# Linear attention and a maxout layer on one core: one transfer for each stored tile, a new order of the last fifth, and a last chunk that is stored by column halves

## The chip, the cores and the metric

The kernel runs on one core of one Trainium2 chip. The time is that of one execution on the device in microseconds (us); several runs are taken, and their median is compared. Besides these runs one execution is recorded by the hardware profiler, and all views shown here come from such records. The engines are TensorE (PE, with its weight loads as PEld), VectorE (DVE), ScalarE (ACT), GpSimd (POOL) and SyncE (SP), which here only issues transfers. The transfers run on 16 DMA engines.

## The reference

Eight batches of eight heads, 576 positions, head dimension 64. First a linear attention with a feature map of 2 x 128 features, then a feed-forward layer with the maximum of three products:

```
def phi(x):
    proj = einsum('bhsd,df->bhsf', x, w_phi)
    proj = proj - max(abs(proj), axis=-1, keepdims=True)
    return concatenate([exp(proj), exp(-proj)], axis=-1)
q_p, k_p = phi(q), phi(k)
kv  = einsum('bhsf,bhsd->bhfd', k_p, v);   z = sum(k_p, axis=2)
num = einsum('bhsf,bhfd->bhsd', q_p, kv)
den = einsum('bhsf,bhf->bhs', q_p, z)[..., None] + 1e-06
x   = (num / den), transposed and reshaped to (4608, 512)
h   = maximum(maximum(x @ w1, x @ w2), x @ w3)     # (4608, 768)
out = h @ w_out                                    # (4608, 512) float32
```

## The kernel before

**Attention** runs over 16 units of four heads (`attention`); two units make a batch. A unit's q, k and v come in as float32 tiles (`raw`), q and k are cast to bf16 (`qk_bf`) and transposed by a DMA (`qkT<-qk_bf`, line 524; in the first units by PE). The row maxima of the q projection, transposed on PE into `mT` (18 rows), are written by a small DMA into a row of `qkT` (`qkT<-mT`, line 582), from where a matmul subtracts them (`psm`, line 626). The divided results (`x_sb`) are transposed by another DMA into `xT` (`xT<-x_sb`, line 703).

**Which token lies where.** A partition holds nine consecutive positions of a batch, so tile c of a batch has the positions 9 i + c for i from 0 to 63. The first eight of the nine tiles of each batch make a chunk of 512 tokens; the ninth tiles of all eight batches are copied by POOL into `x_last` (line 965) and make a ninth chunk. An output tile of 128 rows of chunk b is thus two runs, c = 2 tt and c = 2 tt + 1, of 64 rows each. In the output tensor the rows of a run lie nine rows apart, and the second run starts one row after the first.

**The feed-forward layer** runs over these nine chunks (`chunk`). Differences of the weights are prepared, so that the maximum becomes one relu and one maximum: per chunk twelve groups of matmuls (`ups`, line 848), each taken out of PSUM into `hT` by ACT or DVE. Chunks 0 to 4 then compute each output tile directly (`ops`, lines 879 and 884), copy it to a tile `osb` and store it (line 899). Chunks 5 to 8 (`FAST`) use a scheme with seven products instead of eight (`fast`): POOL forms sums of quarters (line 760), PE the products p1 to p7 (`fps`, line 795), and DVE joins them by additions (`add`, line 802) into two `raw` tiles: `low` holds output rows 0 to 255 of the chunk, `high` rows 256 to 511, each as [128, 2, 512]. In column halves these are the four quarters c11, c12 (low) and c21, c22 (high). They are stored at line 827.

**Stores.** Each stored tile of 128 rows leaves in `n_out` transfers: two of 64 rows in chunks 0 to 7 (one for each run of positions), one of 128 rows in the ninth chunk. SP issues them; in the ninth chunk ACT issues two of the four. SP's queue also carries the loads, the two kinds of transposes and most of the `mT` transfers, in the order in which it issues them.

**The order of all work** is written out by hand: `PLAN` (lines 98 to 253) is a list of steps, each a node's number, a letter for its engine (T PE, D DVE, A ACT, G POOL, S SP) and its buffer slots, with a planned start. `plan` emits each engine's instructions in that order; the planned times set nothing else but the small filler matmuls of the first microseconds (`fill`). PSUM has eight banks, `raw` eight slots; a step that writes a slot waits until the slot's last readers, stores among them, are done.

Of the kernel before, what the change touches and what calls it, by code (L numbers as in the profile page):

```python
# [12 lines left out]
ALU = mybir.AluOpType  # L13
AXX = mybir.AxisListType.X

B, H, S, D = 8, 8, 576, 64
DF = 128
DM = H * D
# [99 lines left out]
199A@37.90 151D1@37.97 194A0@38.05 154T5@38.05 189A@38.30 233T2@38.36 195S@38.45 82D@38.59 180A@38.64 364G@38.78 156T7@38.81  # L118
# [18 lines left out]
318A@67.59 392T4@67.73 1133T@67.79 305D@67.94 393A0@68.08 313A@68.33 321D@68.55 1300G@68.82 1138D3@69.15 414T037@69.19
1134A2@69.34 394A@69.95 559G2@70.02 322T42@70.23 307T16@70.35 882S4@70.50 325D@70.60 415A@70.65 1152T0@70.68 311D@70.94
688S6@70.96 323A@71.05 560G@71.14 687S7@71.42 310D@71.54 1140T3@71.55 308A@71.69 298S1@71.88 326D@72.15 416A@72.18 1127S@72.34
1142T4@72.42 324A@72.64 1141D0@72.67 309A@72.98 306D@73.28 327T7@73.29 1146T1@73.35 328A1@73.60 1153D@73.88 329S@74.00  # L140
330A1@74.03 304A@74.28 432T003200@74.31 333G1@74.43 1147D@74.50 447T67@74.55 558S2@74.70 494G@74.71 433A@74.80 1154T0@74.87
450D@75.11 751S5@75.16 449A@75.29 1143D@75.72 405T10@75.74 448A@75.80 1158T6@75.96 428S3@75.98 406A@76.29 1155D@76.35 407A@76.79
1150T5@76.83 451D@76.97 434A@77.28 1159D@77.58 1148T4@77.70 1151A@77.95 436D@78.20 1144T0@78.57 435D@78.80 411T7@79.44
332G@79.50 1162T1@79.56 413A@79.81 1145A@80.15 1160T6@80.43 1149A@80.65 1163D@80.68 412A@81.15 399T5@81.30 408T0@81.52
1161D@81.55 331G@81.59 402T2@81.74 401A@81.77 1156T3@81.96 561S1@82.21 400A@82.28 403A@82.76 1172T1@82.83 1157D@83.08 404A@83.27
690G1@83.68 409A@83.75 437T47@83.80 452T56@84.04 340T31@84.25 438A@84.29 455D@84.41 1173T@84.47 440D@84.75 454A@84.78 410A@85.12
441D@85.35 686S1@85.57 453A@85.60 349T125@85.86 342A@85.94 1174D1@86.02 1135S@86.03 439A@86.43 456D@86.64 442T40@86.90
341A@86.92 350D@87.15 417T70@87.23 1175S@87.23 443A@87.40 445D@87.53 346T1@87.55 1164T6@87.67 348A@87.92 418D0@88.14 347A@88.28
1139S@88.43 343T2@88.54 351D@88.76 421T3@88.76 754G2@88.93 345A@89.01 334T4@89.08 337T1@89.30 422D1@89.33 356T71@89.52
496S2@89.77 338A@89.77 423T5@89.84 357D0@90.09 1165T@90.16 339A@90.28 446D@90.71 335A@90.76 689G@90.86 344A@91.25 424D1@91.32  # L150
419T3@91.46 336A@91.73 354T1@91.78 420D0@92.03 358T7@92.10 444A@92.22 1168T2@92.42 355D1@92.65 1166A2@92.71 425S@92.97
359D0@93.27 352T4@93.29 460A0@93.32 463A0@93.59 572T110511@93.71 461G@93.72 353D1@93.89 567T63@93.94 562T17@94.18 568A@94.43
1169T@94.51 575D@94.51 360S@94.66 573A@94.92 570D@95.12 569A@95.41 566D@95.72 462G@95.81 574A@95.90 577T40@95.90 881S7@96.16
1176T6@96.23 571D@96.33 1170A1@96.39 621S5@96.62 580D@96.94 579A@97.00 1177T@97.10 563A@97.49 565D@97.55 564A@98.00 576D@98.15
457T3@98.40 582T24@98.55 479T017@98.67 458A0@98.71 581D@98.76 583A@98.96 459S@99.11 584A@99.32 585D@99.37 578A@99.66
502T005300@99.71 586D@99.81 622S1@99.81 1182T2@100.04 481D@100.15 493S3@100.27 590A1@100.30 480D@100.53 1178A3@100.55
591G1@100.70 506D@100.91 512T47@101.01 507T10@101.24 1179S@101.31 515D@101.52 1190T6@101.57 509A@101.73 510D@102.12 504A@102.22
1186T4@102.44 1167S@102.51 514A@102.71 1183D1@102.73 593G@102.79 592G@103.07 508A@103.20 1188T1@103.31 505D@103.34 503A@103.69
511D@103.95 513A@104.18 1200T2@104.18 1189D@104.55 1187A@104.67 467T30@105.05 1465G@105.16 1191A@105.17 1201D@105.30
817S2@105.31 609T150@105.37 1306G@105.56 468A@105.67 469A@106.17 497T12@106.41 517T46@106.64 610A@106.66 625G0@106.76  # L160
1184T3@106.85 500D@106.89 611A@107.06 519A@107.46 516D@107.50 476T0@107.72 587T5@107.84 624G@107.88 1198T1@107.90 477A@108.09
520D@108.11 1185D@108.45 478A@108.45 470T7@108.77 588A1@108.79 464T4@108.99 501D@109.06 589S@109.19 473T0@109.21 471A@109.24
1196T5@109.43 465A@109.73 626S0@109.89 472A@110.21 1202T3@110.30 1197D@110.55 474A@110.70 486T70@111.17 475A@111.20 1203D@111.42
1194T5@111.49 466A@111.69 487D0@112.04 498A@112.17 600T01@112.36 1180T3@112.58 1195D@112.66 499A@112.68 816S1@113.09 602A@113.17
1199D@113.28 522T4@113.45 597T7@113.51 601A@113.68 603T2@113.73 521D@113.90 482T5@113.95 604A@114.20 1181D@114.24 1208T1@114.27
605A@114.71 483D1@114.85 488T0@115.14 525A0@115.19 598A@115.44 594T3@115.46 523D0@115.47 526G0@115.59 1192T5@115.68 489D0@115.71
524S@115.82 518A@115.93 599A@116.27 623S5@116.52 484T2@116.55 596A@116.75 1193D@116.80 1204T4@116.87 1171S@116.98 595A@117.26
485D1@117.42 528G@117.69 637T110611@117.84 527G@117.97 632T75@118.07 1131S@118.18 640D@118.32 532T20@118.40 634A@118.56
541T3@118.62 1209T@118.74 543A@119.05 636D@119.20 542A@119.41 534A@119.75 641D@119.81 606T0@120.04 884G0@120.06 538T3@120.16
533A@120.26 1205T@120.38 691S1@120.41 635D@120.41 540A@120.74 1210D3@121.02 885G@121.18 633A@121.23 529T2@121.68 539A@121.72  # L170
1206D2@121.93 544T071@122.00 530A@122.20 1301G@122.30 531A@122.71 627T53@123.04 545D@123.29 546A@123.29 535T4@123.37
1466G@123.50 1212T2@123.59 490S@123.61 630D@123.67 537A@123.84 1303G@123.90 631D@124.27 536A@124.34 549T71@124.46 547T1@124.78
550D0@125.03 629A@125.03 553T5@125.10 752S3@125.11 551T4@125.42 638A@125.52 548D1@125.65 1213T@125.74 628A@126.01 552D0@126.27
608A@126.50 607A@126.86 554D1@126.89 642T73@127.13 639A@127.20 702T001400@127.37 645D@127.62 555S@127.66 647T05@127.66
704A@127.85 1216T6@127.87 651D@128.22 1214A1@128.34 705D@128.56 614T70@128.74 644A@128.95 1217T@129.06 886S2@129.16 650D@129.17
703A@129.44 615D0@129.51 648A@129.93 706D@130.13 649A@130.29 652T2@130.36 697T10@130.51 1218A0@130.63 653D1@130.74 692T75@130.78
700D@131.00 707T42@131.09 694A@131.27 1230T6@131.42 646D@131.61 699A@131.76 710D@132.21 1222T1@132.29 654S@132.36 655A1@132.36
656G1@132.76 1231D0@132.82 946S7@133.06 1224T4@133.16 1223D@133.43 883S4@133.52 1234T6@134.03 695D@134.04 1225A@134.28
# [123 lines left out]
def kernel(  # L302
# [439 lines left out]
    def fast(b, ready, hT, evac, out_rows, ff, n_out):  # L742
# [268 lines left out]
```

## Time and profile before

| | |
|---|---|
| median of 3 runs | 283.24 us (282.25 to 283.63) |
| profiled execution, its own time | 282.29 us |
| its span, first to last instruction | 280.5 us |
| PE busy | 270.9 us (97%) |
| DVE, ACT, POOL busy | 224.0, 191.3, 168.5 us |
| granted clock of TensorE, mean | 0.996 |
| DMA packets, bytes, mean rate | 68050, 51.46 MB, 183 GB/s |
| stores on SP: `osb` tiles, `raw` tiles of 64 rows | 40 and 24 transfers of 128 KB |
| stores of the ninth chunk | 4 transfers of 256 KB, two on SP and two on ACT |

The span lies inside the time of a run; what is left, 1.8 us, lies around it. A busy PE is one with matmuls in flight, so its share alone does not say that it works at its best. The page cuts the span into 40 slices, one digit for each; 9 means 90% or more. A DMA share is the mean over the 16 DMA engines and can pass 1, since packets overlap. In a row of waits the column after the colon is the total, then how often and the longest.

### The profile page before, as it was taken

The numbers are of one execution on the slowest core, as the hardware profiler recorded it, in microseconds if no ns is written. First come the engines' busy times: TensorE is split into PE (matmuls) and PEld (weight loads), VectorE is DVE, ScalarE is ACT, GpSimd is POOL, SyncE is SP. The second block draws the span as 40 slices with busy tenths as digits, with TensorE's granted clock in tenths as the row PEclk, the third lists the DMA queues.
The fourth block names the chain that finished last, engine by engine and source line by source line (L and its number), as shares of the span: only waits on it lengthen the run. The fifth ranks groups of instructions, "written<-read, shape, count | busy, mean of one in ns | idle before, by whom it ended". The sixth has DMA issues, their size and how long they took to land.

```text
span 280.5 us, 8829 instructions
## 1 busy us (share of the span) xinstructions
PE 270.9 (97%) x3663; PEld 164.1 (58%) x3663; DVE 224.0 (80%) x466; ACT 191.3 (68%) x439; POOL 168.5 (60%) x147
## 2 busy tenths in 40 slices
PE   8899999999999999999999999999999999999991
PEld 3566774465546555564556456565485589444881
DVE  4899899988869997889898878897589565756292
ACT  3799997798879988898684699887654860112000
POOL 8075787839444764570768079267875892927910
PEclk9999999999999999999999999999999999999998
DMA  7999999997999997799899729984232108245037
GB/s 212 234 211 320 266 224 197 384 277 139 287 382 245 197 313 251 193 204 227 240 263 156 194 49 261 202 201 89 51 78 49 40 18 118 55 95 116 0 89 212
DMA packets 68050, 51.46 MB, mean 183 GB/s; under 512 B 48746, under 2 KB 52650, under 8 KB 68010
## 3 DMA queue, kind: packets, MB, share of 16 engines
q1 hardware_dynamic: 63561, 45.41, 66.2%
q0 software_dynamic: 4000, 4.92, 10.3%
q8 instruction: 28, 0.46, 0.6%
q10 hardware_dynamic: 449, 0.57, 0.6%
q14 instruction: 12, 0.10, 0.1%
HBM read 34.64 MB, written 9.44 MB: 157 GB/s over the span
## 4 chain that ended last, share of the span: by engine, by line
PE 78%; DMA 9%; DVE 6%; ACT 3%; issue 1%; POOL 1%; DVEq 0%; POOLq 0%; ACTq 0%
PE ups L848 33%; PE fps L795 8%; PE ops L884 7%; PE psn L673 5%; PE kvps L655 5%; PE ops L879 5%; PE psq L547 5%; PE psm L626 5%; DMA qk_bf<-in_k_dram 3%; DMA qkT<-qk_bf 3%; DMA qkT<-mT 3%; ACT Eq L639 2%; DVE raw L802 2%; PE pm L950 2%; PE tps L509 1%; DVE mqp L566 1%
## 5 line engine op out<-in xcount | busy, mean ns | idle before, releaser
L601 POOL TENSOR_TENSOR vab<-raw,em 128x1152 bf16<-128x1152 f32 (+1 forms) x36 | 68.1, 1906 | 69.4 <-ACT em L597 55.1
L560 ACT ACTIVATE Ek<-psk 128x512 bf16<-128x512 f32 (+1 forms) x160 | 82.2, 568 | 13.8 <-PE psk L547 10.0
L848 PE MATMUL ups<-xT,w_bf 128*128 128x512 bf16 x384 | 90.8, 379 | 0.0
L639 ACT ACTIVATE Eq<-psm 128x512 bf16<-128x512 f32 (+1 forms) x160 | 79.4, 571 | 10.4 <-PE psm L626 9.6
L848 PEld LDWEIGHTS <-w_bf 128*128 128x128 bf16 x432 | 41.0, 98 | 46.4
L566 DVE TENSOR_REDUCE mqp<-psq 128x4 bf16<-128x512 f32 (+1 forms) x80 | 49.2, 634 | 8.4 <-PE psk L547 5.7
L566 DVE TENSOR_REDUCE mk<-psk 128x4 f32<-128x512 f32 (+1 forms) x80 | 48.9, 630 | 1.1 <-ACT Ek L560 0.5
L855 DVE TENSOR_TENSOR hT<-hT,ups 128x512 bf16<-128x512 bf16 x54 | 36.2, 684 | 16.8 <-PE ups L848 13.9
L857 ACT ACTIVATE hT<-ups 128x512 bf16<-128x512 f32 x28 | 16.6, 606 | 30.1 <-PE ups L848 30.0
L680 DVE TENSOR_TENSOR x_sb<-psn,rden 128x320 bf16<-128x320 f32 x64 | 31.5, 492 | 2.2
L492 POOL CAST qk_bf<-raw 128x1152 bf16<-128x1152 f32 x24 | 27.2, 1148 | 5.8 <-DMA qkT<-qk_bf 3.5
L673 PEld LDWEIGHTS <-Eq 128*128 128x128 bf16 x640 | 24.7, 97 | 7.5 <-ACT Eq L639 0.7
L884 PE MATMUL ops<-wout_bf,hT 128*128 128x512 bf16 x120 | 29.1, 379 | 0.0
L673 PE MATMUL psn<-kv_sb,Eq 128*128 128x65 bf16 x640 | 26.8, 194 | 0.5 <-ACT Eq L639 0.5
L547 PE MATMUL psq<-w,qkT 64*128 64x128 bf16 x288 | 24.5, 217 | 1.0 <-DMA qkT<-qk_bf 0.6
L547 PE MATMUL psk<-w,qkT 64*128 64x128 bf16 x288 | 24.1, 217 | 0.2
L547 PEld LDWEIGHTS <-qkT 64*128 64x128 bf16 x576 | 16.6, 94 | 12.7 <-issue 8.9
L626 PE MATMUL psm<-qkT,wphi_m 128*128 128x512 bf16 (+1 forms) x70 | 22.3, 359 | 0.5 <-DMA qkT<-mT 0.3
L879 PE MATMUL ops<-xT 128*128 128x512 bf16 x80 | 20.6, 380 | 0.0
L859 DVE TENSOR_SCALAR hT<-ups 128x512 bf16<-128x512 f32 x26 | 17.5, 684 | 3.8 <-PE ups L848 3.6
L655 PE MATMUL kvps<-vab,Ek 64*128 64x65 bf16 x1152 | 20.2, 190 | 0.0
L655 PEld LDWEIGHTS <-Ek 64*128 64x128 bf16 x1152 | 18.8, 94 | 2.3 <-DVE mk L566 0.4
(97 smaller groups left out, 333.8 us busy)
## 6 DMA issues: line engine op xcount, KB each, us to landing
raw<-in_v_dram SPq DMA_DIRECT2D x16, 576.0 KB
raw<-in_q_dram SPq DMA_DIRECT2D x12, 576.0 KB
raw<-in_k_dram SPq DMA_DIRECT2D x12, 576.0 KB
out_dram<-osb SPq DMA_DIRECT2D x40, 128.0 KB
out_dram<-raw SPq DMA_DIRECT2D x24, 128.0 KB
w_bf<-in_moe_w_dram POOLq DMA_DIRECT2D x3, 768.0 KB, 9.4
qk_bf<-in_q_dram POOLq DMA_DIRECT2D x3, 288.0 KB, 8.2
qk_bf<-in_k_dram POOLq DMA_DIRECT2D x3, 288.0 KB, 9.3
```

The costliest lines, as they stand in the source:

```text
L547: nc.tensor.matmul(ps()[:, i, :], lhsT=cols[r, :], rhs=w2[r, c, :], start=True, stop=True)
L560: nc.scalar.activation(Ek[s]()[:, tiles_of(t0, n), :], of(1), EXP, scale=1.0 - 2.0 * s)
L566: nc.vector.tensor_reduce((mq, mk)[c]()[:, tiles_of(t0, n)], of(c), AXX, ALU.max, apply_absolute_value=True)
L601: (nc.vector if n_.eng == "DVE" else nc.gpsimd).tensor_tensor(vab()[:, g, t0:t1, 0:D], vb()[:, t0:t1, :], em()[:, g, t0:t1].unsqueeze(2).t ...
L626: nc.tensor.matmul(psm()[:, 0:w], lhsT=wphi_m, rhs=rhs, start=True, stop=True)
L639: nc.scalar.activation(Eqb()[s][:, cols], psm()[:, 0:w], EXP, scale=1.0 - 2.0 * s)
L655: nc.tensor.matmul(kvps[ab]()[:, t // NT, g, :], lhsT=Ek[g]()[r, t, :], rhs=vab()[r, g, t, :], start=(t + g == 0), stop=(t == UT - 1 and g ...
L673: nc.tensor.matmul(psn()[:, c, :], lhsT=Eqb()[g][:, t0:t0 + P], rhs=kv()[:, pr, ab, g, :], start=(g == 0), stop=(g == 1))
L848: nc.tensor.matmul(ups(), lhsT=w_bf[i + 1][:, ct, j * P:(j + 1) * P], rhs=tokens_of(ct), start=(ct == 0), stop=(ct == CT - 1))
L855: nc.vector.tensor_tensor(hT()[:, j, :], hT()[:, j, :], ups(), ALU.max)
L879: nc.tensor.matmul(ops_()[:, 0:width], lhsT=tile_of(ct, tt), rhs=line_w[:, ct, cols], start=(ct == 0), stop=False)
L884: nc.tensor.matmul(ops_()[:, 0:width], lhsT=hT()[:, j, tt * P:(tt + 1) * P], rhs=wout_bf[:, j, cols], start=False, stop=(j == JT - 1))
```

## The change

Three parts.

1. Stores of chunks 0 to 7: the two transfers of 64 rows become one of 128 rows, which writes the two runs as [2, 64, 512].
2. The ninth chunk: product p4, which completes c21, is split into its two row tiles, each in a PSUM bank of its own with an addition of its own. Its results leave in five transfers instead of four: c11, c12 and c22 (256 rows of 256 columns each), then the two halves of c21 (128 rows of 256 columns each), dealt to SP and ACT.
3. `PLAN` is new for the last fifth, and slightly so before: three of the `x_last` copies on POOL come earlier (at places planned for 65, 90 and 120 us instead of 105, 124 and 211). From about 238 us on, chunk 7's `ups` groups come before those of chunk 8, ACT takes all twelve relus of the two chunks, and products, additions and stores of both stand in another order.

The code, without the table:

```diff
-        def product(a, w, s):
-            ps = bank("fps", [P, 2, HF])
+        def product(a, w, s, halves=(0, 1)):
+            ps = bank("fps", [P, len(halves), HF])
             def mm(ps=ps, a=a, w=w):
-                for p in range(2):
+                for k, p in enumerate(halves):
                     for c in range(5):
-                        nc.tensor.matmul(ps()[:, p, :], lhsT=a(c, p), rhs=w(c), start=(p + c == 0), stop=(p + c == 5))
+                        nc.tensor.matmul(ps()[:, k, :], lhsT=a(c, p), rhs=w(c), start=(k + c == 0),
+                                         stop=(k == len(halves) - 1 and c == 4))
...
-        p4 = product(a_of(1, 1), t_of(3), None)
-        n_21 = add(lambda: p4, [n_7, n_22], c21, c21, [high])
+        n_21 = []
+        for halves in ((0,), (1,)) if b == B else ((0, 1),):
+            p4 = product(a_of(1, 1), t_of(3), None, halves)
+
+            def c21_of(halves=halves):
+                return high()[:, halves[0]:halves[-1] + 1, 0:HF]
+            n_21.append(add(lambda p4=p4: p4, [n_7, n_22], c21_of, c21_of, [high], 0.07 + 0.28 * len(halves)))
...
-        for tt in range(SM // P):
-            o2, need = (low, [n_11, n_12]) if tt < 2 else (high, [n_21, n_22])
+        parts = [(low, 0, 2, 0, HF, n_11), (low, 0, 2, HF, DM, n_12), (high, 0, 2, HF, DM, n_22),
+                 (high, 0, 1, 0, HF, n_21[0]), (high, 1, 2, 0, HF, n_21[-1])]
+        for o2, p0, p1_, c0, c1, need in parts if b == B else []:
+            def last(n_, o2=o2, p0=p0, p1_=p1_, c0=c0, c1=c1):
+                whole = out.rearrange("(r c) n -> c r n", c=NT)[NT - 1]
+                t0 = HT * (o2 is high)
+                queue_of[n_.eng].dma_start(whole[t0 + p0 * P:t0 + p1_ * P, c0:c1].rearrange("(t p) n -> p t n", p=P),
+                                           o2()[:, p0:p1_, c0:c1])
...
+        for tt in range(0 if b == B else SM // P):
+            o2, need = (low, [n_11, n_12]) if tt < 2 else (high, n_21 + [n_22])
...
-              lambda tt, rows=rows: [(rows[2 * tt + i], slice(i * ST, (i + 1) * ST)) for i in range(2)], 2)
+              lambda tt, rows=rows: [(rows[2 * tt:2 * tt + 2], slice(0, P))], 1)
```

Of the table, one line of the end before and one now:

```diff
-1458D@268.23 1507T6@268.73 1453D@268.85 1464S@269.00 1456D@269.49 1509T5@269.82 1508D3@270.11 1463S@270.20 1512D@270.75
+1511T4@271.10 1510D3@271.66 1522S@271.81 1514T2@272.19 1512D@272.44 1513D@273.15 1516T3@273.28 1518T1@273.82 1515D@273.84
```

SP's queue between the attention of the middle batches and the end, as a difference (a row is the line, what is written and from what, the shape that is written, and how often it stands there in a row):

```order
 L524 DMA_TRANSPOSE qkT<-qk_bf 128x18x128
 L486 DMA raw<-in_v_dram 128x2x576 x2
-L899 DMA out_dram<-osb 64x512 x4
+L915 DMA out_dram<-osb 2x64x512 x2
 L703 DMA_TRANSPOSE xT<-x_sb 128x10x128 x2
 L582 DMA qkT<-mT 1x18x128
```

Nothing has moved against its neighbours; each pair of stores is one, and its shape has a new outermost count of 2. At the queue's end, where only stores are left:

```order
 L703 DMA_TRANSPOSE xT<-x_sb 128x10x128
-L827 DMA out_dram<-raw 64x512 x22
-L827 DMA out_dram<-raw 128x512 x2
+L843 DMA out_dram<-raw 2x64x512 x11
+L834 DMA out_dram<-raw 128x2x256 x2
+L834 DMA out_dram<-raw 128x256
```

Eleven stores of the new shape stand ahead of the three parts of the ninth chunk that SP issues. DVE's last additions, of the ninth chunk, before (osb_5773 is the chunk's intermediate, raw_5731 its `low`, raw_5789 its `high`, each fps a product):

```order
L802 TENSOR_TENSOR osb_5773<-fps_5747,raw_5731 128x512
L802 TENSOR_TENSOR raw_5731<-fps_5735,osb_5773 128x2x256
L802 TENSOR_TENSOR raw_5789<-fps_5762,osb_5773 128x2x256
L802 TENSOR_TENSOR raw_5789<-fps_5735,raw_5789 128x2x256
L802 TENSOR_TENSOR raw_5789<-fps_5778,raw_5789 128x2x256
L802 TENSOR_TENSOR raw_5731<-fps_5793,raw_5731 128x2x256
L802 TENSOR_TENSOR raw_5731<-fps_5808,raw_5731 128x2x256
```

and now (osb_5747, raw_5721 and raw_5761 are the same three tiles):

```order
L803 TENSOR_TENSOR osb_5747<-fps_5725,raw_5721 128x512
L803 TENSOR_TENSOR raw_5721<-fps_5710,raw_5721 128x2x256
L803 TENSOR_TENSOR raw_5761<-fps_5736,osb_5747 128x2x256
L803 TENSOR_TENSOR raw_5721<-fps_5750,osb_5747 128x2x256
L803 TENSOR_TENSOR raw_5761<-fps_5750,raw_5761 128x2x256
L803 TENSOR_TENSOR raw_5721<-fps_5764,raw_5721 128x2x256
L803 TENSOR_TENSOR raw_5761<-fps_5777,raw_5761 128x256
L803 TENSOR_TENSOR raw_5761<-fps_5783,raw_5761 128x256
```

`low`'s left half is now finished second instead of last but one, and the last two additions, into `high`, are halves of what was one.

More of the change, by code (lines that the diff above doesn't have):

```diff
@@ L137 @@
[L137 to L154, printed above, removed]
@@ L248 @@
[L248 to L252 removed]
+381D@61.25 283A@61.50 390D@61.86 282A@61.86 218T0@61.98 1126A1@62.23 278T5@62.30 291T61@62.52 219D1@62.55 289T4@62.84
@@ new lines @@
+441D@85.54 453A@85.79 686S1@85.86 349T125@86.05 342A@86.13 1174D1@86.20 1135S@86.32 439A@86.61 456D@86.82 1175S@86.97
+442T40@87.09 341A@87.10 350D@87.34 417T70@87.42 1139S@87.52 443A@87.59 445D@87.72 346T1@87.74 1164T6@87.86 348A@88.11
+418D0@88.33 347A@88.47 343T2@88.73 351D@88.95 421T3@88.95 345A@89.20 754G2@89.22 334T4@89.27 337T1@89.49 422D1@89.52
+356T71@89.71 338A@89.96 496S2@89.96 423T5@90.03 357D0@90.28 1466G@90.34 1165T@90.35 339A@90.46 446D@90.90 335A@90.95 344A@91.43
+424D1@91.50 419T3@91.65 689G@91.84 336A@91.92 354T1@91.97 420D0@92.22 358T7@92.29 444A@92.40 1168T2@92.61 355D1@92.84
@@ new lines @@
+955D@189.03 1469G@189.04 849S@189.27 969A@189.49 956D@189.64 972T74@189.70 869T153@189.82 1294A3@189.98 975D@190.24
+962T20@190.86 957T61@191.09 870A@191.11 871D@191.11 1338G7@191.20 857T70@191.42 965D@191.49 958A@191.58 863T3@191.64
+1326T5@191.86 960D@192.09 865A@192.11 1336G@192.40 858A@192.60 976D@192.70 1334T2@192.73 961D@193.04 864A@193.08 859A@193.57
+1015G@193.60 1314T6@193.60 966D@193.65 980A0@194.40 860T3@194.47 1322T7@194.69 1315D0@194.72 981G0@194.80 1016S0@194.87
+862A@194.94 1327D@195.35 861A@195.45 1318T6@195.56 1323A@195.93 1320T3@196.43 1319A@196.68 1309G@196.90 963A@197.18
@@ new lines @@
+1312T7@197.30 1321D@197.55 1337G@197.57 866T6@198.17 1330T5@198.29 1313D@198.42 867A@198.54 1311G@198.77 868A@198.90
+1324T3@199.16 1331D@199.41 982G@199.44 854T7@200.03 1335D@200.03 1332T5@200.25 855A@200.50 1325D@200.65 856A@201.01
+1316T6@201.12 1333D@201.37 974A@201.49 1339G@201.53 959A@201.83 1328T7@201.99 1317A@202.32 964A@202.82 876T20@202.86
+1329D@203.11 872T3@203.18 983A@203.31 973A@203.46 878T1@203.50 877D0@203.73 874T6@203.82 1340G3@203.88 1344T5@204.14
+873D1@204.35 875D0@204.97 1357T7@205.23 1345A6@205.48 879D1@205.59 1341G@205.63 880S@206.36 1027T112011@206.42 1022T43@206.65
@@ new lines @@
+1017T61@206.89 1028A@206.90 1030D@206.90 1350T5@207.22 1342G4@207.36 1029A@207.41 1025D@207.51 1299S@207.86 1018A@207.90
+1020D@208.12 977T2@208.31 1346T4@208.37 1295S@208.41 1019A@208.41 1031D@208.72 1024A@208.90 1468G@209.09 1348T6@209.46
+1026D@209.54 1387G1@209.79 1347D0@210.15 1373T0@210.55 1351D@210.79 1343G@210.99 1349D2@211.41 1363T4@211.42 978D1@212.03
+1358D@212.23 1369T6@212.29 979A@212.38 1389G@212.72 1364D1@212.85 1365T2@213.16 1370A@213.41 1352D@213.46 1374D@214.08
+999T074@214.12 1366A@214.28 1021D@214.69 1023A@214.78 1032T56@215.16 1037T20@215.40 1001A@215.41 993T31@215.61 1035D@215.65
@@ new lines @@
+1034A@215.81 1371T1@215.83 1041D@216.25 994A@216.30 1036D@216.59 987T4@216.70 995A@216.81 1381T5@216.92 1040D@217.20
+1372A@217.29 1375T3@217.79 1039A@217.79 1382D@218.04 1045A1@218.13 989A@218.38 1046G1@218.53 1042T1@218.66 1367T2@218.72
+1000A@218.87 1043D0@218.97 1376D@219.17 988A@219.27 1044S@219.32 984T5@219.59 1377T7@219.81 1368A@219.84 1291S@220.02
+985A@220.34 1047G@220.62 990T4@220.68 986A@220.84 1355T1@220.90 1378D@220.93 992A@221.33 996T3@221.99 1385T2@222.11 1356D@222.24
+998A@222.36 1048A@222.70 1471G@222.72 997A@222.85 1379T5@222.98 11G@223.12 991A@223.19 1386D@223.23 1388G@223.27 1033A@223.67
@@ new lines @@
+1072D1@231.62 1074D0@232.24 1067T7@232.46 1397T1@232.78 1068D1@233.03 1075S@233.80 1408T5@233.87 1395T3@234.96 1401T2@236.05
+1396D0@236.30 1398D2@236.93 1404T7@237.14 1472G@237.23 1409D@237.57 1438G7@237.63 1400D4@238.19 1414T3@238.23 1403D@238.83
+1439G@238.85 1416T1@239.10 1415A0@239.35 1407D@239.47 1426T5@239.97 1440G@240.05 1402D@240.10 1417A@240.22 1413S@240.25
+1418T0@240.84 1427D@241.09 1441G@241.25 1405D@241.71 1428T3@241.71 1419A@241.96 1497G5@242.45 1411S@242.48 1420T6@242.58
+1429D@242.83 1410S@243.03 1430T2@243.45 1412S@243.58 1498G@243.67 1421A@243.70 1422T1@244.32 1431D@244.57 1499G@244.87
@@ new lines @@
+1432T5@245.19 1423A@245.44 1424T7@246.06 1500G@246.07 1433D@246.31 1434T0@246.93 1425A@247.18 1473T3@247.80 1435D@248.05
+1436T6@248.67 1474A1@248.92 1475T2@249.54 1437D@249.79 1354D@250.41 1485T1@250.41 1442G1@250.56 1476A@250.66 1359S@251.18
+1477T5@251.28 1486D@251.53 1360S@251.73 1487T7@252.15 1361S@252.28 1443G@252.31 1478A@252.40 1479T0@253.02 1488D@253.27
+1489T3@253.89 1445G3@254.06 1480A@254.14 1481T6@254.76 1490D@255.01 1491T4@255.63 1444G@255.79 1482A@255.88 1483T2@256.50
+1492D@256.75 1493T1@257.37 1484A@257.62 1446T5@258.24 1494D@258.49 1495T7@259.33 1447A0@259.58 1448T0@260.20 1496D@260.45
@@ L787, in fast, with add @@
         base = ready + evac + lines + [w_nodes[3]] + t_made
-        def product(a, w, s):
-            ps = bank("fps", [P, 2, HF])
+        def product(a, w, s, halves=(0, 1)):
+            ps = bank("fps", [P, len(halves), HF])
             def mm(ps=ps, a=a, w=w):
-                for p in range(2):
+                for k, p in enumerate(halves):
                     for c in range(5):
-                        nc.tensor.matmul(ps()[:, p, :], lhsT=a(c, p), rhs=w(c), start=(p + c == 0), stop=(p + c == 5))
+                        nc.tensor.matmul(ps()[:, k, :], lhsT=a(c, p), rhs=w(c), start=(k + c == 0),
+                                         stop=(k == len(halves) - 1 and c == 4))
             need = [] if s is None else [made[0, s], made[1, s]]
-            n_ = ff("fp", {"PE": 1.09}, mm, base + need, [hT, ps] + ([] if s is None else [Sx, Sr[s // 2]]))
+            n_ = ff("fp", {"PE": 0.545 * len(halves)}, mm, base + need, [hT, ps] + ([] if s is None else [Sx, Sr[s // 2]]))
             readers[b].append(n_)
             return ps, n_
-        def add(ps, need, out, other, bufs):
-            return ff("fa", {"DVE": 0.62}, lambda: nc.vector.tensor_tensor(out(), ps()[0](), other(), ALU.add),
+        def add(ps, need, out, other, bufs, dve=0.62):
+            return ff("fa", {"DVE": dve}, lambda: nc.vector.tensor_tensor(out(), ps()[0](), other(), ALU.add),
                       need + [ps()[1]], [ps()[0]] + bufs, locks=[ps()[0]])
@@ L817, in fast @@
         n_12 = add(lambda: p3, [n_w], c12, c12, [low])
-        p4 = product(a_of(1, 1), t_of(3), None)
-        n_21 = add(lambda: p4, [n_7, n_22], c21, c21, [high])
+        n_21 = []
[4 more added lines that the diff above has]
+            n_21.append(add(lambda p4=p4: p4, [n_7, n_22], c21_of, c21_of, [high], 0.07 + 0.28 * len(halves)))
         p2 = product(a_of(0, 1), b_of(1, 0), None)
         n_11 = add(lambda: p2, [n_u], c11, c11, [low])
-        for tt in range(SM // P):
-            o2, need = (low, [n_11, n_12]) if tt < 2 else (high, [n_21, n_22])
+        parts = [(low, 0, 2, 0, HF, n_11), (low, 0, 2, HF, DM, n_12), (high, 0, 2, HF, DM, n_22),
[6 more added lines that the diff above has]
+                                           o2()[:, p0:p1_, c0:c1])
+            n_ = ff("store", {"SP": 0.6, "ACT": 0.6}, None, [need], [o2], pipe=0.5 * (p1_ - p0), lat=1.5, packet=100.0)
+            n_.fn = lambda n_=n_, f=last: f(n_)
+        for tt in range(0 if b == B else SM // P):
+            o2, need = (low, [n_11, n_12]) if tt < 2 else (high, n_21 + [n_22])
             def store(n_, pieces, tt=tt, o2=o2):
```

186 lines of the change are left out of this document (84 added, 102 removed).

## The prediction

> **What bounds the kernel now.** I read the page first, then stretches of the span, the chain of waits, the DMA queues and, last, single transfers. The page's strips and its first queue:
>
> ```profile
> PE 270.9 (97%) x3663; PEld 164.1 (58%) x3663; DVE 224.0 (80%) x466; ACT 191.3 (68%) x439; POOL 168.5 (60%) x147
> ...
> PE   8899999999999999999999999999999999999991
> ...
> DMA  7999999997999997799899729984232108245037
> ...
> q1 hardware_dynamic: 63561, 45.41, 66.2%
> ```
>
> TensorE (PE) is busy in every slice until the last. The DMA engines are nearly full for the first two thirds, idle in the middle of the last third, and full again at the end. Four stretches (span, busy time of PE, PEld, DVE, ACT, POOL, then clock, DMA share, GB/s):
>
> ```profile
> 73.00:195.00 122.00, 121.10 (x1744) 68.68 (x1743) 105.05 (x223) 101.68 (x235) 68.09 (x55) 1.00 0.92 221
> 195.00:240.00 45.00, 45.00 (x547) 30.84 (x546) 32.57 (x66) 24.32 (x55) 33.03 (x28) 1.00 0.34 61
> 240.00:275.00 35.00, 34.59 (x230) 22.25 (x228) 22.02 (x36) 5.24 (x9) 19.84 (x15) 1.00 0.35 79
> 276.00:278.50 2.50, 0.00 (x0) 0.00 (x0) 0.00 (x0) 0.00 (x0) 0.00 (x0) 0.93 1.03 393
> ```
>
> PE stands still for under 1 us between 73 and 195 us, though the DMA engines have only 8% to spare there. The one long wait in that stretch is for a transfer, with nothing between its landing and PE (chain of waits):
>
> ```profile
> 120.22 7.68 DMA qkT<-qk_bf
> 127.91 0.05 issue
> 127.95 0.23 PE psq L547
> ```
>
> So PE bounds the kernel, and the transfers follow close behind. After PE's last product DVE has the tail, then the last stores (timelines of DVE, of the queue SP, and the queue's wait at the end):
>
> ```profile
> 265.96 0.69 DVE L802 TENSOR_TENSOR osb<-fps,raw 128x512 f32<-128x512 f32 x1 [5.33 <-PE fps L795]
> ...
> 272.65 2.68 DVE L802 TENSOR_TENSOR raw<-fps,raw 128x512 f32<-128x512 f32 x4
> 240.79 35.05 SPq L827 DMA_DIRECT2D out_dram<-raw  x24
> ...
> SPq L1006 <- DMA out_dram<-raw: 3.2, 1, 3.2
> ...
> DMA  6999999899999899999979999989999999984310
> ```
>
> DVE sat idle for 5.33 us, then worked with hardly a gap until 275.33. The last row is the DMA strip from 276 to 278.8 us: the data of the last stores ran until 278.8, and the span ends 1.7 us later.
>
> **What a store costs: on how many DMA engines does it run?** This decides the forecast. Today a stored tile is two transfers of 64 rows. A stretch from 241.8 to 243.4 us that holds two of them and nothing else:
>
> ```profile
> DMA  0019199947992779035999290979277963130000
> ...
> DMA packets 160, 0.26 MB, mean 164 GB/s; under 512 B 32, under 2 KB 32, under 8 KB 160
> ```
>
> 128 packets are rows of 2 KB; the other 32, tiny, are completions: 16 for each transfer, one for each DMA engine that took part. A stretch that holds a single transfer of 18 rows of 256 B (mT into qkT, 4.5 KB):
>
> ```profile
> DMA packets 27, 0.00 MB, mean 15 GB/s; under 512 B 27, under 2 KB 27, under 8 KB 27
> ```
>
> Here 18 are rows, which leaves 9 completions: nine engines with two rows each, not sixteen. So a transfer is cut into equal parts, and their number, 16 at most, divides a count in its shape: 16 for 64, 9 for 18. The new store writes [2, 64, 512] (two runs of 64 rows that can't be joined in the output) from 128 rows. If the count is the outermost one, as the cut of both sides in step needs, it is 2 there against 128, and the store runs on two engines. If it is the number of rows, 128, it still runs on 16. No row of this trace has two sides of different shape, so this is read from one shape, not shown. I take two engines.
>
> The Trainium skill ("DMA: Bandwidth & Descriptors", section "Why a DMA increments its semaphore by 16 and not by 1") states it as a rule: the engines used are the largest number up to 16 that divides the slowest dimension, other than 1, of both sides, and they are the lowest-numbered ones; the nine completions agree. The same page ("Bandwidth") advises larger transfers, which taken alone favours this change. By the first rule the time is the forecast below, by the second the sixteen-engine rival.
>
> **The change, part by part.** *Price of a store on two engines.* In the saturated stretch all 16 moved 393 GB/s, so one moves 24.6; a tile of 256 KB gives each of two engines 128 KB, 5.3 us. Today it gives each of sixteen 16 KB, 0.67 us. No row shows a DMA engine faster than that, and 16 of them reach it together, so I take it for one engine's own pace.
>
> *The stretch from 73 to 195 us.* What it moves (DMA issues there):
>
> ```profile
> DMA packets 40195, 26.98 MB, mean 221 GB/s; under 512 B 31683, under 2 KB 31683, under 8 KB 40177
> ...
> raw<-in_v_dram SPq DMA_DIRECT2D x10, 576.0 KB
> out_dram<-osb SPq DMA_DIRECT2D x34, 128.0 KB
> raw<-in_q_dram SPq DMA_DIRECT2D x7, 576.0 KB
> raw<-in_k_dram SPq DMA_DIRECT2D x6, 576.0 KB
> qkT<-mT SPq DMA_DIRECT2D x9, 4.5 KB
> qkT<-qk_bf SPq DMA_TRANSPOSE x9
> xT<-x_sb SPq DMA_TRANSPOSE x9
> ```
>
> Two quiet stretches, of 3.8 and 2.4 us, hold one large and one small transpose and each the edge of another transfer:
>
> ```profile
> DMA packets 2390, 0.71 MB, mean 188 GB/s; under 512 B 2336, under 2 KB 2336, under 8 KB 2390
> ...
> DMA packets 1365, 0.43 MB, mean 181 GB/s; under 512 B 1313, under 2 KB 1313, under 8 KB 1365
> ```
>
> That is about 3.3 us for a large transpose and 1.9 for a small one, without the edges. The 34 half stores become 17; on each of the two engines they need 17 x 5.3 = 91 us. The rest at undisturbed prices: 23 loads x 1.5 (36 KB at 24.6 GB/s) = 34; nine large and nine small transposes, 47. Together 91 + 34 + 47 = 172 us of work on two engines in 122 us: 50 too much. All of it lies in SP's queue, in order: every load and transpose has a share on those two engines, behind the stores. An example (SP):
>
> ```profile
> 86.53 4.06 SPq L899 DMA_DIRECT2D out_dram<-osb  x6
> 90.69 3.88 SPq L524 DMA_TRANSPOSE qkT<-qk_bf  x1
> 94.67 1.37 SPq L703 DMA_TRANSPOSE xT<-x_sb  x1
> ```
>
> Those six become three of 16 us together, and the transposed qk and xT behind them land some 14 us later; PE, without slack, waits. Ends for this term: 0 if early loads cover everything, and 70 if the share stands as measured (0.92 x 122 = 112, less 34 x 8 KB at 24.6 GB/s = 11, plus 91, less 122). I take 50, the sum by undisturbed prices, since a contended packet's time contains waiting. From 195 to 240 us the four stores there (21 us at a share of 0.34) fit.
>
> *The tail.* The queue then has eleven stores in a row, the first issued at 240.79 today, and the last chunk's parts behind them. On two engines: 240.8 + 50, 1.1 from issue to first data (the strip of the two 64-row stores begins at 241.9), 11 x 5.3 = 58.7, the last chunk's 640 KB on this queue over sixteen engines 1.6, and 1.7 from last data to the end: 353.9. PE and DVE are done earlier, though delayed: the add that opens the upper half of chunk 7 reuses a tile whose store is the seventh of the eleven, so it waits for it.
>
> *The rest* rests on four rows (stores on SP, the copies on POOL, POOL's longest wait, a half-wide DVE copy from PSUM):
>
> ```profile
> L899 SPq DMA_DIRECT2D out_dram<-osb x40: 467/589/1467, 73.8 to 220.8; - x40
> ...
> L965 POOL COPY x_last<-xT x8: 395/397/403, 104.7 to 238.6; 128x256 bf16<-128x256 bf16 x8
> ...
> POOL vab L601 <- ACT em L597: 55.1, 12, 9.5
> ...
> L660 DVE CAST kv_sb<-kvps 128x260 bf16<-128x260 f32 x16 | 6.4, 423 | 2.3 <-PE kvps L655 2.2
> ```
>
> SP issues 32 stores fewer, 0.59 us each; today its issues hide behind PE. Three x_last copies on POOL move earlier, 0.40 us each; POOL waits for ACT for 55 us in all, which hides them (without that cover 1.2 us). DVE's work on chunk 7 starts earlier, so its 5.33 us of idle time is used, but chunk 8's adds still wait for PE, whose matmuls are the same in number: DVE would end near 275.3 as now. Halving one add costs at most one add (0.69) and at least nothing; the nearest row, DVE copying 128x260 from PSUM at 0.42, gives 2 x 0.42 - 0.69 = +0.15.
>
> The last stores' rows of 1 KB cost between half a 2 KB packet and a whole one; they leave on sixteen engines either way. All this is under 2 us, and without effect where the two engines end last.
>
> *Sum.* The profiled execution took 282.29 us for a span of 280.5. The span grows by 50 + 23.4 to 353.9; with 1.8 around it 355.7. The median of the runs is 1 us above that execution: 356 to 357.
>
> **The rivals.** One row for the third of them, the first matmuls of the span (shortest, median, longest in ns):
>
> ```profile
> L979 PE MATMUL idler<-idle x27: 379/389/634, 1.0 to 15.2; 128*128 128x512 bf16 x27
> ```
>
> (1) *Sixteen engines*: the count is rows. For it: the trace has no counter-example. Then the tail alone changes. PE ends as now, the last add near 275.3, its 128 KB is issued at once, first data 1.1 later, 0.7 for it and its neighbour, 1.7 to the end: 278.8 instead of 280.5, or 281.5 on the median's footing: faster. This rival is the other sign, and it decides if a store shows 16 completions. (2) *Two engines, but the stretch before 195 us is covered* by early loads, or the pair rotates so that stores overlap: the tail alone, 282.3 + 23.4 = 306. Against it: PE's slack of 0.9 us in 122. (3) *Each wait adds* to the engines' load: 70 instead of 50 gives 376, and PE restarting slowly after waits, as in its first matmuls (634 ns for what takes 379 later), would add more; I put the end at 395, an estimate from these two.
>
> **How the numbers follow.** Forecast (two engines, both delays, 325 to 385): 0.66; covered (300 to 325): 0.12; worse than 385: 0.07; sixteen engines: 0.15. 0.5% (1.4 us) is about what a measurement tells from no change. Of the last case 0.10 is faster, 0.04 same, 0.01 slower; all else is slower. The range 304 to 395 leaves out the sixteen-engine case and the far ends, together under 0.2.
>
> **What would show it.** Right: 128 rows and 2 completions in a store's packets; a DMA share near 0.13 and some 49 GB/s for tens of us at the end, with PE and DVE done; PE waiting from the first stores on (75 to 100 us) for qkT<-mT, qkT<-qk_bf and xT<-x_sb; store landings some 5 us apart. Wrong: 16 completions a store and landings as now. The size is wrong if PE waits start only after 130 us, or if the strip shows the two engines idle between stores.

## The result: a third slower, and the profile after

The changed kernel takes 378.53 us (median of 4 runs, 374.72 to 378.71) against 283.38 us before: 1.334 times the time, with a 95% interval of 1.326 to 1.342. The forecast was 356 us, its range 304 to 395. The profiled execution took 374.72 us for a span of 372.9, so it is the shortest of the runs shown; its mean granted clock was 0.902, that of the others 0.884 to 0.889. Ratios here and below compare the runs in the chip's faster state alone, while the medians are of all runs, a few slow ones included.

The page of the changed kernel, the rows that answer to those of before: busy time, the strips of PE, of its granted clock and of the DMA engines, and the first queue.

```profile
PE 285.7 (77%) x3628; PEld 169.4 (45%) x3663; DVE 223.1 (60%) x462; ACT 195.7 (52%) x444; POOL 168.5 (45%) x147
...
PE   8999999999566859399926397955997988997400
...
PEclk9999999999786969879995889996999998999955
DMA  8999997999199947784298137997121091111132
...
q1 hardware_dynamic: 63001, 45.54, 56.5%
```

PE had no slice below 8 before the end; now it has holes from the eleventh slice (93 us) on, and stands still for the last two. The same bytes cross, but the DMA strip ends in a long row of ones.

The two completions that the prediction asked for can be read directly. From 289.2 to 296.2 us a single store runs (DMA view of that window):

```profile
DMA  0201010130012011110111111111111111110300
...
DMA packets 131, 0.28 MB, mean 40 GB/s; under 512 B 2, under 2 KB 2, under 8 KB 130
```

There are 128 rows of 2 KB, one block of instructions, and two tiny packets: two engines took part. Its data alone needs 6.3 us. In the long row of stores at the end, from 320 to 350 us:

```profile
DMA  1111111111111112111111111111111111111111
GB/s 49 55 49 49 55 49 52 52 49 55 49 49 55 49 52 74 49 52 52 49 55 49 49 55 49 49 55 49 55 49 49 55 60 49 55 49 52 52 49 52
```

The plateau of 49 to 55 GB/s fits two of sixteen engines (two sixteenths of the 393 GB/s of before are 49); queued stores land 5.13 us apart (327.91, 333.04, 338.16 us and so on). They follow each other instead of running side by side, and it is the same two engines each time. The packets of the ninth chunk's parts on SP show it: of their 640 rows of 1 KB, 560 moved from 362.3 to 365.4 us beside a store, and the last 80, the share of two engines out of sixteen, only from 369.6 us on, behind the last row of the eleven stores. That is the rule of the Trainium skill ("DMA: Bandwidth & Descriptors", section "Why a DMA increments its semaphore by 16 and not by 1"), which names the lowest-numbered engines; the trace does not give their numbers.

What stands behind such a store is seen in SP's timeline (start, length) and in the chain of waits:

```profile
90.71 3.55 SPq L915 DMA_DIRECT2D out_dram<-osb  x3
94.35 15.43 SPq L524 DMA_TRANSPOSE qkT<-qk_bf  x1
109.88 3.57 SPq L703 DMA_TRANSPOSE xT<-x_sb  x2
```

```profile
90.71 8.69 DMA out_dram<-osb
...
111.35 4.17 DMA xT<-x_sb
...
125.89 9.05 DMA qkT<-mT
```

Before, the issue of this transpose into qkT took 3.88 us; here SP is held in it for 15.43 us, the time that the three stores ahead of it need (their data runs from 93.8 to 109.3 us). All later loads and transposes wait with it. PE's waits for those transfers, DVE's one wait for a store in the tail, and the waits of ACT for a slot of `osb` whose store isn't done (total, times, longest):

```profile
PEld L626 <- DMA qkT<-mT: 26.8, 7, 8.2
PE psm L626 <- DMA qkT<-mT: 24.6, 6, 8.0
PEld L547 <- DMA qkT<-qk_bf: 22.4, 4, 10.3
PE psq L547 <- DMA qkT<-qk_bf: 21.6, 3, 10.2
...
DVE raw L803 <- DMA out_dram<-raw: 10.7, 1, 10.7
...
ACT osb L908 <- DMA out_dram<-osb: 8.2, 3, 5.8
```

PE and PEld wait at the same time, so PE's share of each pair of rows is one of the two. The first of its long stops, at 96 us, goes through the last row: a product has to wait for ACT's copy, and that for the store on the two engines (the 8.69 us in the chain above). The stages (span, busy time of PE, PEld, DVE, ACT, POOL, then clock, DMA share, GB/s); the first one ends where the stretch of before ended, one microsecond into the last transpose into qkT (193.97 us before, 258.10 now):

```profile
73.00:259.10 186.10, 133.26 (x1719) 72.82 (x1739) 106.70 (x224) 103.08 (x236) 67.77 (x54) 0.86 0.76 146
259.10:308.00 48.90, 45.17 (x545) 30.89 (x547) 32.67 (x67) 24.61 (x57) 30.44 (x24) 1.00 0.33 55
308.00:355.00 47.00, 37.65 (x232) 23.14 (x233) 19.66 (x31) 8.34 (x14) 22.38 (x17) 0.96 0.14 49
355.00:371.00 16.00, 0.00 (x0) 0.00 (x0) 0.16 (x1) 0.00 (x0) 0.00 (x0) 0.50 0.30 106
```

### The profile page after: what moved, and what is told of

Its sections match the earlier page's. It is cut to its first block, busy times and chain, and to the rows that moved or that the text cites. A ratio compares the mean times of both kernels' runs of the same rounds, so it can differ in the third digit from the quotient of the medians.

```text
span 372.9 us, 8768 instructions
## 1 busy us (share of the span) xinstructions
PE 285.7 (77%) x3628; PEld 169.4 (45%) x3663; DVE 223.1 (60%) x462; ACT 195.7 (52%) x444; POOL 168.5 (45%) x147
## 4 chain that ended last, share of the span: by engine, by line
PE 48%; DMA 32%; ACT 3%; DVE 3%; issue 3%; SPq 3%; POOL 2%; DVEq 0%; POOLq 0%; ACTq 0%
PE ups L864 21%; DMA qkT<-mT 11%; DMA qkT<-qk_bf 7%; DMA out_dram<-raw 5%; PE ops L900 5%; PE psm L626 4%; PE kvps L655 4%; DMA qk_bf<-in_k_dram 4%; PE ops L895 4%; PE psq L547 3%; PE psn L673 3%; DMA xT<-x_sb 3%; DMA out_dram<-osb 2%; PE fps L795 2%; ACT Eq L639 2%
## 5 line engine op out<-in xcount | busy, mean ns | idle before, releaser
L864 PE MATMUL ups<-xT,w_bf 128*128 128x512 bf16 x368 | 94.8, 396 | 5.6 <-DMA xT<-x_sb 4.5
L864 PEld LDWEIGHTS <-w_bf 128*128 128x128 bf16 x432 | 42.5, 101 | 55.3 <-issue 11.2
L547 PE MATMUL psq<-w,qkT 64*128 64x128 bf16 x288 | 26.8, 229 | 26.0 <-DMA qkT<-qk_bf 21.6
L626 PE MATMUL psm<-qkT,wphi_m 128*128 128x512 bf16 (+1 forms) x70 | 24.2, 387 | 25.1 <-DMA qkT<-mT 24.6
L873 ACT ACTIVATE hT<-ups 128x512 bf16<-128x512 f32 x33 | 19.6, 604 | 31.9 <-PE ups L864 31.7
L900 PE MATMUL ops<-wout_bf,hT 128*128 128x512 bf16 x114 | 31.5, 414 | 0.5 <-issue 0.3
L547 PE MATMUL psk<-w,qkT 64*128 64x128 bf16 x288 | 26.4, 229 | 0.2
L875 DVE TENSOR_SCALAR hT<-ups 128x512 bf16<-128x512 f32 x21 | 14.3, 685 | 19.6 <-PE ups L864 19.3
L626 PEld LDWEIGHTS <-wphi_m 128*128 128x128 bf16 x70 | 6.6, 101 | 32.8 <-DMA qkT<-mT 26.8
L760 POOL TENSOR_TENSOR raw<-hT 128x768 bf16<-128x768 bf16 x8 | 13.1, 1639 | 17.1 <-DVE hT L871 10.7
```

The source lines that it names most:

```text
L547: nc.tensor.matmul(ps()[:, i, :], lhsT=cols[r, :], rhs=w2[r, c, :], start=True, stop=True)
L626: nc.tensor.matmul(psm()[:, 0:w], lhsT=wphi_m, rhs=rhs, start=True, stop=True)
L864: nc.tensor.matmul(ups(), lhsT=w_bf[i + 1][:, ct, j * P:(j + 1) * P], rhs=tokens_of(ct), start=(ct == 0), stop=(ct == CT - 1))
L900: nc.tensor.matmul(ops_()[:, 0:width], lhsT=hT()[:, j, tt * P:(tt + 1) * P], rhs=wout_bf[:, j, cols], start=False, stop=(j == JT - 1))
```

## The experiments

**Which part of the change costs the time?** The changed kernel with two stores of 64 rows again (the new order, the split p4 and the column halves stay), and the kernel before with the one-transfer store alone.

```diff
-              lambda tt, rows=rows: [(rows[2 * tt:2 * tt + 2], slice(0, P))], 1)
+              lambda tt, rows=rows: [(rows[2 * tt + i], slice(i * ST, (i + 1) * ST)) for i in range(2)], 2)
```

> The changed kernel, but chunks 0 to 7 store each tile again in two transfers of 64 rows; the new order and the column halves stay. Theory A (a store that writes [2, 64, 512] runs on two DMA engines, and everything behind it in SP's queue waits): the slowdown is gone whole, and what is left is the tail of the sixteen-engine rival, 283.4 - 1.7 = 281.7 us, ratio 0.994. Rival B (the new order makes PE wait for transfers): over 340 us still. Rival C (a mixture): in between, above 290.

Measured: 282.15 us (12 runs) against 283.56, ratio 0.993 (0.990 to 0.997).

> The kernel before with one edit: one transfer [2, 64, 512] for each tile of chunks 0 to 7, nothing else. Theory A: all of the slowdown, 370 to 384 us, 2 completions by engines for a store, PE waits from 80 us on. Rival B (the new order): 283 us. Rival C: between 290 and 360.

Measured: 379.84 us in one run. So the one-transfer store is the whole slowdown, and the rest of the change is a small gain of 0.7%.

**Is it the size of the transfer or the shape that it writes?** The changed kernel, still with one transfer of 128 rows, but its output side written as [64, 2, 512] instead of [2, 64, 512]. The bytes, the packets and the source are the same; within each tile the rows land in another order, so the output is permuted.

```diff
-              lambda tt, rows=rows: [(rows[2 * tt:2 * tt + 2], slice(0, P))], 1)
+              lambda tt, rows=rows: [(rows[2 * tt:2 * tt + 2].rearrange("c i n -> i c n"), slice(0, P))], 1)
```

> The changed kernel with still one transfer of 128 rows and 256 KB for each tile, but with the two counts in the output exchanged: [64, 2, 512] instead of [2, 64, 512]. The rows of a tile come to lie in another order among the same 128 output rows, which is all that differs in the result. Theory A (the outermost count sets the number of engines): 64 and 128 give sixteen, 16 completions a store, 281 to 282 us as with the pairs. Rival D (one large transfer is slow, whatever its shape, or strided runs are): over 340 us.

Measured: 281.8 us, ratio 0.994 (0.992 to 0.997). A stretch with one such store and nothing else (243.8 to 245.4 us):

```profile
DMA packets 144, 0.26 MB, mean 164 GB/s; under 512 B 16, under 2 KB 16, under 8 KB 144
```

Sixteen completions, and its data took 0.8 us. One transfer instead of two does no harm; the outermost count of 2 does all of it.

**Does the count set the number of engines in between?** The kernel before, its two stores of 64 rows written as [4, 16, 512] (again permuted within the tile).

```diff
-              lambda tt, rows=rows: [(rows[2 * tt + i], slice(i * ST, (i + 1) * ST)) for i in range(2)], 2)
+              lambda tt, rows=rows: [(rows[2 * tt + i].rearrange("(a b) n -> b a n", b=4), slice(i * ST, (i + 1) * ST)) for i in range(2)], 2)
```

> The kernel before with its pairs of 64-row transfers, each with its 64 output rows written as [4, 16, 512] (4 rows of stride one beside each other outermost; rows land in another order among the same 64). Theory A: four engines, 4 completions by engines for a transfer, 2.6 us on each of the four for a tile instead of 5.1 on two: in the stretch from 73 to 195 us 17 x 2.6 = 44 us on top of 81 (undisturbed) to 101 (by the share) in 122, so 3 to 23 us of delay, and some 10 at the end for the stores of chunks 6 and 7: 293 to 315 us. Rival D (only the size of a transfer matters): 283 us. A rule that only two is slow: 283 us.

Measured: 317.18 us in one run, a little above what was expected. A pair of stores alone, 248.1 to 252.2 us:

```profile
DMA packets 136, 0.26 MB, mean 64 GB/s; under 512 B 8, under 2 KB 8, under 8 KB 136
```

Eight completions for two transfers: four engines each. Outermost counts of 2, 4, 18 and 64 thus gave 2, 4, 9 and 16 engines. That the time is higher than the engines' work suggests is taken up below.

**Do the two delays add?** The kernel before with one-transfer stores for chunks 0 to 4 alone, and for chunks 5 to 7 alone.

```diff
+ [(rows[2 * tt:2 * tt + 2], slice(0, P))] if b < FAST[0] else [... two of 64 rows ...]
```

> The kernel before, with the one-transfer store for chunks 0 to 4 alone (the 20 stores of osb tiles); chunks 5 to 7 keep two stores of 64 rows. If the two delays add, as forecast, this run shows the first alone. By the forecast's size (50 us) 283 + 50 = 333. By the size read from the changed kernel's trace (the transpose into qkT that stands at 193.97 us goes to 258.1, and the transposes into xT behind it are 65 to 71 us late) 283 + 64 to 71, 347 to 355. A rival: the end of the kernel takes up part of the delay, so that the first part alone costs less than 50 and both parts together only look additive; then below 330.

> The kernel before, with the one-transfer store for chunks 5 to 7 alone (12 stores of raw tiles, eleven of them in a row at the end). If the delays add, this shows the tail alone: 240.8 + 1.1 + 11 x 5.13 + 1.6 + 1.7 = 301.6 for the span by the queued store's 5.13 us, 303.4 with what lies around it, and one more where a store stands alone: 303 to 307. If the tail's cost was partly hidden behind the delay of the first part, more than 310.

Measured: 353.77 and 309.29 us, beside 281.67 for the kernel before (one run each): 72 and 28 more. Together they are 100, and both at once cost 95 (changed kernel) and 96 to 98 (the store alone), so they add but for a few us (2 to 5, with one run of each). The early size is that of the trace, not that of the forecast, and the last transpose into qkT stands at 258.27 us, as in the changed kernel. The late one came 2 us above its expected range. Its eleven stores are one at 242.4 us (6.2 us of data) and ten in a row from 249.4 us; those and the ninth chunk, in this kernel still four whole tiles, need 56.3 us, where 10 x 5.13 + 1.6 = 52.9 were counted.

**Is it the two engines or the order of SP's queue?** The 20 stores of `osb` tiles issued by ACT instead of SP, once as one transfer each, once (the control) as two of 64 rows.

```diff
         n.eng, n.start = {"T": "PE", "D": "DVE", "A": "ACT", "G": "POOL", "S": "SP"}[what[at]], float(start)
+        n.eng = getattr(n, "queue", n.eng)
...
+                n_.queue = "ACT"
```

> The kernel before with the one-transfer stores in all chunks, but the 20 stores of osb tiles issued by ACT instead of SP, at the same places of the plan. It tells apart why the stretch of the first stores grows. If the two DMA engines' own work is the limit, it matters little who issues: 17 x 5.25 us of stores, 82 us of loads and transposes and the 14 us without any packet stay, and the time is within 10 us of 380. If it is the order of SP's queue, in which loads and transposes stand behind stores, the waits shrink: without the 14 us 366, with the stores out of the way altogether down to 306. If ACT is held up while it issues, more than 390; the control is the next kernel.

> The control: the kernel before, its 40 stores of 64 rows of osb tiles issued by ACT instead of SP. ACT was busy for 102 of 122 us in that stretch; 40 issues of about 0.55 us each are 22 us more over the span. If they fit into its idle time, 283 to 286; if ACT becomes the limit there, up to 295, and the kernel with one transfer on ACT must be read against this one.

Measured: 371.92 us, and 288.32 us for the control. The control costs 6.6 us, so issuing on ACT is not free. Against it the two-engine stores add 83.6 us, where they added 96 to 98 on SP. At the end of the stretch that holds 17 of these 20 stores, the last transpose into qkT is 50.3 us later than in the control (249.35 against 199.02 us); with all stores on SP it was 63.6 us later than in the kernel before (257.59 against 193.97). So the order of SP's queue is worth some 13 us of the 64, and 50 remain although no load or transpose of SP stands behind one of these stores in its own queue: most of it is the two engines, which both queues share. SP was still held for 12.11 us in the issue of one transpose (96.05 us), where the longest in this stretch of the control was 4.25. ACT's own issues explain little: two of them took 5 us each, all others about 0.6 at most. The Trainium skill ("DMA: Bandwidth & Descriptors", section "Queues, rings and completion order") says the same of the two queues: each has a ring on every one of the same sixteen engines, and an engine takes turns between the rings. The changed kernel's trace agrees: from 357.6 to 360.4 us, packet by packet, two rows of ACT's part of the ninth chunk and two rows of a store from SP alternate, 48 of each, again the share of two engines (ACT's other 336 rows had moved by 356.3 us). The 13 and the 50 us put sizes to the sharing.

**Where does the small gain of the other parts come from?** The changed kernel with two stores of 64 rows, its ninth chunk leaving as before in four whole tiles.

```diff
-        parts = [(low, 0, 2, 0, HF, n_11), (low, 0, 2, HF, DM, n_12), (high, 0, 2, HF, DM, n_22),
-                 (high, 0, 1, 0, HF, n_21[0]), (high, 1, 2, 0, HF, n_21[-1])]
...
-        for tt in range(0 if b == B else SM // P):
+        for tt in range(SM // P):
```

> The changed kernel with two stores of 64 rows for each tile and with the ninth chunk's results leaving as before, as four whole tiles of 128 rows (two on SP, two on ACT); the new order and the split p4 stay. With two stores of 64 rows and the column halves the kernel took 0.66% less than before (281.7 against 283.6). In the traces its last addition ended at 274.8 instead of 275.3 us, and the time from there to the end of the span was 3.7 instead of 5.2 us. If these two readings are right, the order alone gives 0.5 us and the column halves 1.5: here 283.0 (ratio 0.998). If the order gives the gain and the halves nothing: 281.7 (0.993). If whole tiles behind the new order come late as one block: above 283.6.

Measured: 281.92 us, ratio 0.9965 (0.993 to 0.9999): between the two readings. So both kernels were run again side by side.

> The changed kernel with two stores of 64 rows, once more, beside the next kernel on one chip, so that the column halves alone are told apart. If they give the 1.5 us that the traces show between the last addition and the end, this kernel is 0.5% faster than the next and 0.7% than before (281.6 for a before of 283.5).

> The same with the ninth chunk leaving as four whole tiles, in the same minutes on the same chip. If the halves carry the gain, 0.998 of before (283.0); if the new order carries it and the halves nothing, the two agree within 0.2%, both near 0.994.

Measured: 280.89 us with the halves, ratio 0.992 (0.990 to 0.994), and 282.42 us with whole tiles, ratio 0.997 (0.996 to 0.999). The halves give about 0.5%, the new order with the split p4 about 0.3%. The last additions and the DMA strip from 274 to 281.5 us, first with the halves, then with whole tiles:

```profile
272.91 2.00 DVE L803 TENSOR_TENSOR raw<-fps,raw 128x512 f32<-128x512 f32 x4
...
DMA  0008999999999993000000000000000000000000
...
DMA packets 832, 0.79 MB, mean 105 GB/s; under 512 B 64, under 2 KB 832, under 8 KB 832
```

```profile
274.77 2.00 DVE L803 TENSOR_TENSOR raw<-fps,raw 128x512 f32<-128x512 f32 x4
...
DMA  0000000000000002999999999999995000000000
...
DMA packets 576, 1.05 MB, mean 140 GB/s; under 512 B 64, under 2 KB 64, under 8 KB 576
```

With whole tiles 1.05 MB are left to write in one burst, and the span ends 4.7 us after the last addition (281.5); with the halves 0.79 MB, and 3.7 us (278.6). In these two profiles the additions also ended 1.9 us apart, more than the medians of the runs differ (1.5), so a single profile isn't the measure here. The kernel with two stores of 64 rows and column halves is the fastest seen that computes the reference.

## Why the prediction was right in its mechanism and 22 us short

**The step that decided it** was right: a store of [2, 64, 512] runs on two engines. It had been read from the nine completions of the 18-row transfer; the two completions of the store, the eight of two [4, 16, 512] stores and the sixteen of a [64, 2, 512] store show it. In the row of stores the DMA share was 0.14 at 49 GB/s, where 0.13 and 49 were asked. One sign beside it came only late: PE and DVE were to be done in that row, but they ended at 351.6 and 355.2 us, when some 42 and 45 of its 63 us had passed. The rival of sixteen engines is thereby out, and so is the rival of a covered middle: PE's waits began at 96 us, within the 75 to 100 that the forecast asked. Their first cause, the slot of `osb`, had not been named in it.

**The price of a store** was right: 5.3 us were taken. Between 73 and 259.1 us some store's rows are moving for 89.3 us, 17 x 5.25. A store alone took up to 6.4 us, a queued one 5.13.

**The sum of the stretch** is the term that was too small: 50 us of delay forecast, 64.1 measured (the transpose that stood at 193.97 us is at 258.10). Its 186.1 us can be split by the packets in the trace (by time, since the trace has no numbers of engines; time with both kinds counts for the stores): 89.3 with rows of a store (forecast 91), 82.4 with other packets only (forecast 81 for loads and transposes), and 14.4 without any packet (forecast none). So both works were priced within 2 us, and the step that failed is the last one: 172 us of work was set equal to 172 us of time, as if the two engines never stood empty. That the two engines stand idle between stores is what the prediction itself had named as a sign of a wrong size. One of these empty times, from 254.9 to 260 us in the changed kernel, just ahead of the last transpose into qkT:

```profile
DMA  9920000000000000000000000000000000299999
GB/s 295 276 23 0 0 0 0 0 0 0 0 0 0 0 0 0 0 0 0 0 0 0 0 0 0 0 0 0 0 0 0 0 0 0 38 195 225 213 213 221
```

SP waits here for POOL's cast of the input of that transpose (4.8 us by the waits). The kernel before has the same gap at the same place (191 to 195.2 us), there with 3.5 us of waiting for the cast:

```profile
DMA  7100000000000000000000000000000000000001
```

It has 13.1 us without a packet in its 122. In the sum they were taken as free for the stores, and the share of 0.92 hid them, since overlapping packets count twice. They weren't to be had: in some 8 of the changed kernel's 14.4 us SP waits before it can issue, for the cast above or for other results, and in the other 6 it is issuing and no data has started. Two other kernels agree. With one-transfer stores for chunks 0 to 4 alone the stretch is 186.3 = 88.7 + 83.5 + 14.1. With [4, 16, 512] stores it is 145.4 = 52.9 + 82.4 + 10.0 (rounded), where the method of the forecast gives 17 x 2.67 + 81 = 126; here 10 of the 19 us that are missing are empty time, and 8 are that a tile took 3.1 us instead of 2.67. In the kernel with the stores on ACT the empty time falls to 7.6 us of 177.4, in the direction of the smaller delay there; its other parts can't be compared, since transfers of the two queues mix (106.9 us with rows of a store, 62.9 with others only). The other end of that term, 70 from the measured DMA share, was nearer: its 112 us of share for what the forecast priced at 92 held some 20 us of contended packets, about as much as the gaps that it left out too. It was near by that accident; its split was no better.

**From 195 to 240 us** no delay was forecast, since four stores of 21 us fit into a share of 0.34. They do fit, but the first data of the tail came at 309.8 us instead of 241.9, 67.9 later, so 3.8 us were added here. Transfers that stand behind these stores on SP are the likely reason; no experiment singles it out.

**The tail** was right: from its first data to the end of the span 62.0 us were forecast (58.7 + 1.6 + 1.7), 63.1 measured. The reused tile held up DVE's additions for 10.7 us as foreseen, behind stores that were slower still. The three differences, 14.1 + 3.8 + 1.1, are the 19.0 us by which the span of 372.9 exceeds the forecast 353.9; the rest of the 22 is that the median of the runs lies 3.8 us above the profiled execution, not 1. Those runs also had the lower granted clock (0.884 to 0.889 against 0.902); whether the clock made them longer isn't shown.

**The small parts** were right to 1 us: without the two-engine stores the other edits gain 0.7%. Forecast for that case (the sixteen-engine rival) was 281.5, measured 282.15 and, in the second run, 280.89 with two stores of 64 rows, and 281.8 with one of [64, 2, 512].

**The third rival**, in which PE restarts slowly, holds in part. PE's granted clock fell to 0.86 in the stretch with waits, and its products there took longer (the group of `ups`, busy time and mean ns of one: before and after over the whole span, then after in that stretch alone):

```profile
L848 PE MATMUL ups<-xT,w_bf 128*128 128x512 bf16 x384 | 90.8, 379 | 0.0
```

```profile
L864 PE MATMUL ups<-xT,w_bf 128*128 128x512 bf16 x368 | 94.8, 396 | 5.6 <-DMA xT<-x_sb 4.5
```

```profile
L864 PE MATMUL ups<-xT,w_bf 128*128 128x512 bf16 x183 | 49.4, 402 | 2.4 <-DMA xT<-x_sb 1.6 <-issue 0.4
```

All of PE was busy for 14.8 us more in the span. How much of that lay on the path wasn't tried; the accounts of the packets close without it, though a slower PE may be part of the time without packets.

## What to carry to other kernels

Before transfers are merged, look at the outermost dimension of both sides of the new one: in these runs it alone set the number of DMA engines, and 256 KB took 0.8 us with 64 outermost and 5.1 to 6.4 us with 2. The completions in a quiet stretch of the trace tell the number of engines without an experiment. When the work of a resource is summed against a stretch, the time in which it stood empty before belongs in the sum unless it can be shown to be free: here 13 us stood empty between dependent transfers before the change, and 14 after it.

## What was not expected of the hardware

- SP was held in the issue of one transpose for 15.43 us behind three stores on two engines; in the kernel before the longest was 6.2 us.
- Stores on two engines delayed transfers of another queue most of the way: 50.3 us in the first stretch with the stores on ACT, 63.6 with them on SP.
- A store on two engines moved at 41 GB/s alone (256 KB in 6.35 us) and at 51 in a row of them (5.13 us).
- Where a store on two engines met the rows of a sixteen-engine transfer from another queue, the packets of the two queues alternated strictly, two and two: 48 rows of each in 2.9 us, after the other engines' share of that transfer had landed 1.3 us earlier.
- The granted clock of PE was 0.86 in a stretch in which it was busy for 72% of the time, and 1.00 in the next, in which it was busy for 92%.
